# Attention, mixture of experts and SwiGLU: the low parts of the expert weights from the tenth tile on, on VectorE instead of GpSimd

## The chip, the cores and the metric

The kernel runs on one core of a Trainium2 chip. The metric is the device time of one execution in microseconds (us); the number for a version is the median of its runs. TensorE multiplies matrices, VectorE, ScalarE and GpSimd work on tiles element by element; GpSimd also issues the indirect transfers (gather and scatter), SyncE most of the plain ones. Each engine takes its instructions strictly in the order of its own queue, and waits for others by semaphores.

## The reference

Three stages in float32, the last with float64 weights:

```python
def reference(q, k, v, moe, moe2):          # q, k, v: 4 x 8 heads x 576 x 64
    scores = q @ k.T / 8                    # only the 64 latest positions of each row
    attn = softmax(where(mask, scores, -1e9)) @ v
    x = attn.reshape(2304, 512)
    noisy = x @ w_gate + log1p(exp(x @ w_noise)) * noise      # 8 experts
    top2 = two largest of noisy, w = softmax(top2)
    for e in range(8):                      # w1[e]: 512 x 1024, w2[e]: 1024 x 512
        for each token with e among its two:
            out[token] += w * (maximum(x[token] @ w1[e], 0) @ w2[e])
    g = out @ moe2_w_gate                   # 512 x 1536, float64 weights
    return (silu(g) * (out @ moe2_w_val)) @ moe2_w_out
```

## The kernel before

**Products in two parts.** Every large product is made of three faster ones. A number is split into a high part, rounded to the matrix format, and a low part, the remainder: high times high, high times low, low times high. So every weight tile of 128x1024 is loaded (tile `raw`, three buffers, L101), its high part copied (L116 on ScalarE, or L114 on GpSimd for the first nine), and its low part subtracted (L117). Both parts lie in a tile `wp` of nine buffers. There are 82 weight tiles: eight for each expert (four of w1, four of w2, tiles 0 to 63) and 18 of the last layer (tiles 64 to 81).

**The parts of the program.** Attention and routing come first; the first tiles are split in it. Then the expert layers (L849 to L904): the experts in turn, 0 to 7, the fullest first after expert 0, each with at most 640 to 576 token slots (`CAPS`). Then the last layer, SwiGLU, over 18 tiles of 128 tokens (L920 to L998).

**One expert.** `mm1` (L236) makes the hidden layer: for each f of 0 to 7, and for each of the two halves of the slots (256, then the remaining 320 to 384), twelve products (L248) into one of four PSUM banks, taken in turn. ScalarE writes the high part of the result (`ht`, L250) and VectorE the low part (L253); the bank is free for the fourth product group after it when both are done. `mm2` (L259) follows, five tiles t of 128 slots, 24 products each (L270). Between the tiles the gathered tokens of the next expert are turned, and their two parts written (L230 ScalarE, L233 VectorE).

**What is woven in.** The loop at L859 calls, after every `mm1` of one half, `decode_some(DEC1)`: one step of the decoding of the float64 weights of the last layer, of which there are seven for each half tile, all on VectorE (L143 to L157). After each f it calls `pump` (L169), which splits one more weight tile if a buffer has come free: in an expert's `mm1` this is so at f = 0 to 5 and 7, and once at the end of `mm2`, after t = 4. After each tile of `mm2`, `decode_some(DEC2)` gives six steps of decoding. In expert 0 steps of the routing (`finish_some`) stand where the decoding stands in the others; decoding runs in experts 1 to 6. At the start of an expert GpSimd gathers the next one's tokens (five transfers, L213), and in experts 1 to 3 it scatters 18 routing records, one after each f (L842, L843).

**What ties the splitting to the loads.** `split_pair` first asks for loads up to two tiles ahead, and a load waits in SyncE's queue until its `raw` buffer is free, that is until the low part of the tile three earlier has been subtracted.

The lines that the prediction speaks of are those of `split_pair` and these, from `mm1`'s caller:

```python
                    mm1(e, f, hf)()
                    if e:
                        decode_some(DEC1)
...
                pump()
```

Of the kernel before, what the change touches and what calls it, by code (L numbers as in the profile page):

```python
# [7 lines left out]
F32 = mybir.dt.float32  # L8
# [6 lines left out]
ALU = mybir.AluOpType  # L15
# [6 lines left out]
E = 8  # L22
# [4 lines left out]
KT = CT + 1  # L27
NW = 9
APAIRS = 8
# The slots of the first expert and of the others, the fullest first.  # L30
CAPS = (CAP, 640, 624, 608, 600, 592, 584, 576)
OFFS = tuple(sum(CAPS[:r]) for r in range(E + 1))
EARLY = 2
# [3 lines left out]
RNS, RNS2, RNS3, RT = 1300, 500, 1500, 13  # L37
NWARM, PSPL = 7, 9
EVP = {16: "da", 17: "da"}
# The steps after the last scores, in order: L logits, Q their turn, P turn of the weights, V weighted sum, X turn  # L40
# of x (each with its tile); G turn of gathered tokens, M first product, Y part of the second; W low parts; E, R
# routing on TensorE and VectorE.
TAIL = ("P16", "L14", "Q14", "R302", "X15", "R1500", "G0", "P17", "V16", "L15", "G1", "W", "V17", "Q15", "R9000", "X16",
        "M0", "L16", "X17", "R9000", "R500", "Q16", "R1", "R2500", "L17", "M2", "W", "R500", "M1", "Q17", "W", "M3",
        "R1500", "E", "R700", "M5", "M6", "M4", "R9000", "E", "W", "R9000", "Y0", "Y1", "M7")
# [8 lines left out]
def tile_attention_moe_swiglu(ctx: ExitStack, tc: tile.TileContext, qh, kh, vh, wgn, noise, w1h, w2h,  # L54
                              wg2, wv2, wo2, out):
    nc = tc.nc
# [12 lines left out]
    def bank(i, name, shape=None):  # L69
        return ps.tile(shape or [128, 512], F32, name=name, tag=f"b{i}")  # L70

# [1 line left out]
    srcs = []  # L73
    for r in range(E):
        srcs += [(r, w, j) for w in (w1h, w2h) for j in range(4)]
# [8 lines left out]
    NPAIR, WLIM = len(srcs), 8 * E + 6  # L84
# [3 lines left out]
    def load_pair():  # L88
        j = st["load"]
        if j >= NPAIR:  # L90
            return
        st["load"] += 1
        raws[j] = rp.tile([128, 1024], F32, name=f"raw{j}", tag="raw")
        src = srcs[j]
        if j < 8 * E:
            r, w, i = src
            if r and r not in rank_e:
                rank_e[r] = nc.values_load(rank_i[0:1, r:r + 1], engines=(mybir.EngineType.SP,), min_val=0,
                                           max_val=E - 1)
            src = w[bass.ds(rank_e[r], 1), i].rearrange("o p c -> p (o c)") if r else w[0, i]  # L100
        nc.sync.dma_start(raws[j], src)  # L101

    def split_pair(pool):
        j = st["split"]
        if j >= NPAIR:
            return
        while st["load"] < min(j + 3, st["lim"]):
            load_pair()
        st["split"] += 1
        w = pool.tile([128, 2, 1024], F32R, name=f"wp{j}", tag="w")  # L110
        pairs[j] = w
        r = raws.pop(j)
        if st["split"] <= PSPL:
            nc.gpsimd.tensor_scalar(w[:, 0, :], r, 1.0, 0.0, op0=ALU.mult, op1=ALU.add)  # L114
        else:
            nc.scalar.activation(w[:, 0, :], r, AF.Copy)  # L116
        (nc.gpsimd if j < WLIM or j % 2 else nc.vector).tensor_tensor(w[:, 1, :], r, w[:, 0, :].bitcast(F32), op=ALU.subtract)  # L117

    # The float64 weights of the last layer, rounded to float32 from their bits.
    TINY = 1.125 * 2.0 ** -15  # L120

    def decode_steps(pool):
# [46 lines left out]
    def pump():  # L169
        if st["split"] < min(st["used"] + NW - 1, st["lim"], WLIM):  # L170
            split_pair(wp)

# [1 line left out]
    nc.scalar.preload_act_table_set("natural_log_exp_and_others")  # L174
    init = rp.tile([128, 1024], I32, name="init", tag="raw")
    warm = nc.const_aps.tensor(1.0, (128, 1), BF)
# [80 lines left out]
    Y = {}  # L257
# [19 lines left out]
    def idx_x(e):  # L277
        return lambda t: idx_i[:, e * KT + t:e * KT + t + 1]

    # =============== attention and routing ===============  # L280
    with ExitStack() as ac:
        ap = ac.enter_context(tc.tile_pool(name="ap", bufs=1))

# [21 lines left out]
        Q, K, V, VW = {}, {}, {}, {}  # L305
# [291 lines left out]
        routing, at = [], {}  # L597

        def step():
            g = routing[0]  # L600
            at[g] = next(g, "end")
            if at[g] == "end":
                routing.pop(0)
            return at[g]

        def route_some(ns):
            """Emits routing steps of about ns on VectorE, and none that another engine has yet to answer."""
            while routing and ns > 0:
                r = step()
                if r in ("act", "pe", "dve"):  # L610
                    return
                if r != "end":
                    ns -= r if isinstance(r, int) else 220
# [29 lines left out]
        for T in range(NT - 2):  # L643
            trans_p(T)
            qk(T + 2, (0, 1))
            if T % 2 == 0 and T // 2 + 2 < NT // 2:
                load_super(T // 2 + 2)
            route_some(RNS if T < RT else RNS3)
            if T >= 2:
                logits(T - 2)  # L650
            if T >= 1:
                trans_x(T - 1)
            if T % 2 == 1 and T // 2 + 2 < NT // 2:
                link_k(T // 2 + 2)
            route_pe()
            route_some(RNS2 if T < RT else RNS3)
            qk(T + 2, (2,))
            if T >= 2:
                gates(T - 2)
            qk(T + 2, (3,))  # L660
            softmax(T + 2)
            pv(T)
            win_v(T + 2)
            route_pe()
            if T >= 3 and st["split"] < APAIRS:
                split_pair(wp)
        while routing:
            route_until("end")
        ops = {"L": logits, "P": trans_p, "Q": gates, "X": trans_x, "V": pv, "G": filler, "M": lambda f: filler(f + EARLY),
               "W": lambda _: lows(), "R": route_some, "E": lambda _: route_pe(),  # L670
               "Y": lambda k: mm2(0, k // 4, hp_, "xg", range(2 * (k % 4), 2 * (k % 4) + 2))}
        for op in TAIL:
# [12 lines left out]
        nc.vector.tensor_copy(pos_c, pos_ps)  # L685
        nc.scalar.preload_act_table_set("sigmoid_and_others")

    # =============== expert layers ===============
    GY, XC, X2 = {}, {}, {}

    def gather(T, g0, g1, slots, rows):
# [26 lines left out]
    def finish(pool):  # L718
        V = nc.vector

        def ft(name, shape, dt=F32):
            return pool.tile(shape, dt, name=name)

        def wide(a, shape):
            return a.to_broadcast(shape)

        # The experts but the first in the order of their tokens, the fullest first: isr[r, e].
        key = ft("key8", [128, E])
        V.scalar_tensor_tensor(key, cnt, float(E), kb, op0=ALU.mult, op1=ALU.add)
        yield  # L730
        isr = ft("isr", [128, E, E])
# [7 lines left out]
                        op=ALU.is_equal)  # L739
# [15 lines left out]
        yield  # L755
        V.tensor_copy(idx_i.rearrange("p (e t) -> p e t", t=KT)[:, 1:, 0:CT], idm[:, 1:])
        yield "idx"
        # Too many tokens for an expert's slots?
        V.tensor_tensor(tmp, isr, wide(cnt[:, None, :], [128, E, E]), op=ALU.mult)
        yield  # L760
        ovr = ft("ovr", [128, E])
# [6 lines left out]
        yield  # L768
        V.tensor_tensor(cnt_i, cm[0:1, :], few[0:1, :], op=ALU.max)
        yield  # L770
        # The tokens in the order of the last layer: those of the last expert come after the others, the last tile
        # stays in its place.
        big = ft("big", [128, NT, E])
        lastp, lasto = ft("lastp", [128, NT]), ft("lasto", [128, NT])
        for src, dst in ((pos_c, lastp), (ohs, lasto)):
# [13 lines left out]
        yield  # L789
        V.tensor_copy(ord_i[:, NT - 1:NT], rec[:, NT - 1:NT, 4])  # L790
        yield
        # Slots.
        off = ft("off", [128, E])
        V.tensor_tensor(tmp, isr.rearrange("p r e -> p e r"), wide(offs[:, None, :], [128, E, E]), op=ALU.mult)
        yield
# [3 lines left out]
        for c in range(2):  # L799
            V.tensor_tensor(big, wide(io8[:, None, :], [128, NT, E]), wide(mf_all[:, :, c:c + 1], [128, NT, E]),  # L800
                            op=ALU.is_equal)
# [25 lines left out]
    with ExitStack() as mc:  # L827
# [3 lines left out]
        dec.append(decode_steps(mp))  # L831

        st_, fin = [], finish(mp)

        def finish_some(n):
# [69 lines left out]

    outer.close()

    # =============== SwiGLU ===============
    with ExitStack() as sc:
        sp = sc.enter_context(tc.tile_pool(name="sp", bufs=1))  # L910
        ep = sc.enter_context(tc.tile_pool(name="ep", bufs=len(m2) - NW))
# [8 lines left out]
        while st["split"] < WLIM:  # L920
            split_pair(wp)
# [4 lines left out]
        for bk in range(NBK):  # L926
# [18 lines left out]
            for h in range(2):  # L945
                ut = sp.tile([128, 2, 6, NB2], F32R, name=f"ut{bk}_{h}", tag="ut")
                for fi in range(6):
                    f = 6 * h + fi
                    gb = []
                    for kind in ("g", "v"):  # L950
                        w = pairs[mi[kind, f // 2]].rearrange("p s (k f) -> p s k f", k=NK)
# [26 lines left out]
                order = [(fi, i) for i in range(3) for fi in range(6)] if end else \  # L978
                    [(fi, i) for fi in range(6) for i in range(3)]
                for fi, i in order:  # L980
                    f = 6 * h + fi
                    w = pairs[mi["o", f // 2]].rearrange("p s (c d) -> p s c d", c=2)
# [14 lines left out]
                for i in range(3):  # L997
                    put_out(i)  # L998

    # =============== an expert with more tokens than its slots: every token through every expert ===============  # L1000
    fp = ctx.enter_context(tc.tile_pool(name="fp", bufs=1))
    rv = nc.values_load(cnt_i[0:1, 0:1], min_val=0, max_val=8 * N)
    with tc.If(rv > 0):
# [105 lines left out]
```

## Time and profile before

| what | us |
|---|---|
| median of three runs | 1088.21 |
| the three runs | 1087.7, 1088.21, 1090.81 |
| profiled execution: span, first to last instruction | 1084.2 |
| TensorE busy (matmul) | 1027.2 (95%) |
| VectorE busy | 609.1 (56%) |
| ScalarE busy | 340.2 (31%) |
| GpSimd busy | 334.5 (31%) |
| L117, low parts, on GpSimd | 185.2 in 76 instructions |
| L117, low parts, on VectorE | 7.4 in 6 instructions |

Of the profiled execution the profile gives the span only; the median of the runs is 4.0 us above it. The profile's views give, for a stretch or an instruction, the start in us from the span's beginning, the duration, the engine (PE is TensorE, DVE VectorE, ACT ScalarE, POOL GpSimd, SPq SyncE's queue), the line, and the tile written and read. Idle time before an instruction is put down to what ended it. A duration includes whatever the instruction stood still for after it had started.

### The profile page before, as it was taken

To read this page: it belongs to the slowest core of one execution; us is meant where nothing else is said; L and a number is where in the kernel's file an instruction comes from. 1 tells how busy PE (TensorE), PEld (TensorE's weight loads), DVE (VectorE), ACT (ScalarE), POOL (GpSimd) and SP (SyncE) were. 2 spreads that over 40 slices of the span, in tenths; PEclk is the share of its full clock that TensorE was granted. 3 is DMA by queue.
4 is the path that set the end of the run, shared out by engine and by line. 5 is a ranking of instruction groups with operands and counts; after the bars stand their busy time and mean duration, and the time that the engine had idled before them with its cause. 6 is when DMAs were issued, how large, how long until landed. Compare 5 with 4: busy or idle time off the path is not lost.

```text
span 1084.2 us, 16995 instructions
## 1 busy us (share of the span) xinstructions
PE 1027.2 (95%) x6754; PEld 917.8 (85%) x6754; DVE 609.1 (56%) x1094; ACT 340.2 (31%) x808; POOL 334.5 (31%) x293
## 2 busy tenths in 40 slices
PE   8978999799797999989899999999999999999997
PEld 5656788789687888888879799999999999999996
DVE  4688846878889697888924253433424324324321
ACT  6856524423323242333324162212212212212211
POOL 2653115935717063452708153300300201100000
PEclk9989999999998999999999999999999999999999
DMA  7853115747566375655616162200200201100000
GB/s 240 299 187 99 60 53 191 232 123 244 137 197 198 135 247 167 209 175 188 218 59 191 68 217 79 88 1 1 88 1 1 88 1 34 56 1 2 29 1 32
DMA packets 55774, 125.63 MB, mean 116 GB/s; under 512 B 9144, under 2 KB 19512, under 8 KB 55688
## 3 DMA queue, kind: packets, MB, share of 16 engines
q1 hardware_dynamic: 40695, 87.72, 25.5%
q0 software_dynamic: 7936, 23.91, 6.9%
q10 hardware_dynamic: 7056, 12.85, 3.2%
q8 instruction: 55, 0.90, 0.3%
q14 instruction: 32, 0.25, 0.1%
HBM read 95.57 MB, written 28.88 MB: 115 GB/s over the span
## 4 chain that ended last, share of the span: by engine, by line
PE 80%; DVE 14%; ACT 2%; DMA 1%; issue 1%; SPq 1%; POOL 0%; ACTq 0%; DVEq 0%
PE y L270 20%; PE g L958 14%; PE v L958 14%; PE o L986 14%; PE h L248 12%; DVE da L143 2%; PE gt L228 2%; PE xp L445 1%; DVE da L153 1%; DVE db L151 1%; DVE db L155 1%; DVE ht L253 1%; DVE da L157 1%; DVE da L145 1%; PE sc L404 1%
## 5 line engine op out<-in xcount | busy, mean ns | idle before, releaser
L117 POOL TENSOR_TENSOR wp<-raw,wp 128x1024 fp32r<-128x1024 f32 x76 | 185.2, 2447 | 249.0 <-ACT wp L116 241.9
L248 PE MATMUL h<-xh,wp 128*128 128x256 f32 (+6 forms) x1536 | 229.8, 310 | 29.0 <-DVE ht L253 28.8
L248 PEld LDWEIGHTS h<-xh,wp 128*128 128x128 f32 x1536 | 222.5, 195 | 35.7 <-DVE ht L253 34.1
L270 PE MATMUL y<-wp,ht 128*128 128x512 f32 (+6 forms) x960 | 228.9, 394 | 0.0
L270 PEld LDWEIGHTS y<-wp,ht 128*128 128x128 f32 (+6 forms) x960 | 172.4, 183 | 40.5
L958 PE MATMUL g<-x,wp 128*128 128x384 f32 x864 | 161.6, 334 | 0.0
L958 PE MATMUL v<-x,wp 128*128 128x384 f32 x864 | 161.3, 334 | 0.0
L986 PE MATMUL o<-wp,ut 128*128 128x512 f32 x648 | 153.6, 392 | 0.0
L958 PEld LDWEIGHTS g<-x,wp 128*128 128x128 f32 x864 | 151.3, 188 | 1.0
L958 PEld LDWEIGHTS v<-x,wp 128*128 128x128 f32 x864 | 150.8, 188 | 0.0
L986 PEld LDWEIGHTS o<-wp,ut 128*128 128x128 f32 x648 | 120.4, 188 | 24.1
L963 DVE TENSOR_TENSOR eg<-g,eg 128x384 f32<-128x384 f32 x72 | 40.2, 558 | 151.8 <-ACT eg L962 151.7
L693 POOL DMA_INDIRECT gy<-y_d,recp x30 | 28.7, 955 | 214.3 <-DVE xc L700 206.5
L116 ACT ACTIVATE wp<-raw 128x1024 fp32r<-128x1024 f32 x73 | 76.7, 1055 | 54.8 <-DMA raw<-in_w_dram 37.7
L250 ACT ACTIVATE ht<-h 128x256 fp32r<-128x256 f32 (+7 forms) x128 | 52.7, 421 | 113.3 <-PE h L248 107.1
L966 ACT ACTIVATE ut<-u 128x384 fp32r<-128x384 f32 x72 | 37.9, 526 | 148.2 <-DVE u L965 148.2
L253 DVE SCALAR_TENSOR_TENSOR ht<-h,ht 128x256 fp32r<-128x256 f32 (+7 forms) x128 | 59.1, 465 | 35.6 <-ACT ht L250 35.5
L274 ACT ACTIVATE ys<-y 128x512 f32<-128x512 f32 (+6 forms) x40 | 23.9, 597 | 171.2 <-PE y L270 129.9
L965 DVE TENSOR_TENSOR u<-v,eg 128x384 f32<-128x384 f32 x72 | 40.2, 558 | 62.8 <-PE v L958 62.1
L962 ACT ACTIVATE eg<-g 128x384 f32<-128x384 f32 x72 | 35.3, 490 | 125.7 <-PE g L958 125.7
L233 DVE TENSOR_TENSOR xh<-gt,xh 128x512 fp32r<-128x512 f32 (+6 forms) x40 | 25.7, 662 | 70.5 <-ACT xh L230 70.5
L967 DVE TENSOR_TENSOR ut<-u,ut 128x384 fp32r<-128x384 f32 x72 | 40.9, 568 | 43.0 <-ACT ut L966 43.0
(184 smaller groups left out, 1023.0 us busy)
## 6 DMA issues: line engine op xcount, KB each, us to landing
raw<-in_w_dram SPq DMA_DIRECT2D x64, 512.0 KB, 4.2
w_d<-da ACTq DMA_DIRECT2D x36, 256.0 KB, 3.5
raw<-w_d SPq DMA_DIRECT2D x18, 512.0 KB, 3.4
y_d<-ys SPq DMA_DIRECT2D x34, 256.0 KB, 2.2
rd<-in_wg_dram SPq DMA_DIRECT2D x12, 512.0 KB, 4.7
rd<-in_wv_dram SPq DMA_DIRECT2D x12, 512.0 KB, 4.4
rd<-in_wo_dram SPq DMA_DIRECT2D x12, 512.0 KB, 4.0
v<-in_v_dram SPq DMA_DIRECT2D x18, 256.0 KB, 6.2
```

What stands on the lines that cost most here:

```text
L116: nc.scalar.activation(w[:, 0, :], r, AF.Copy)
L117: (nc.gpsimd if j < WLIM or j % 2 else nc.vector).tensor_tensor(w[:, 1, :], r, w[:, 0, :].bitcast(F32), op=ALU.subtract)
L248: nc.tensor.matmul(b_, w[:, a, k, fc], xh[:, c, k, 0:m], start=(n == 0), stop=(n == 11))
L250: nc.scalar.activation(ht[:, 0, f, 0:m], b_, AF.Relu)
L253: nc.vector.scalar_tensor_tensor(ht[:, 1, f, 0:m], b_, 0.0, ht[:, 0, f, 0:m].bitcast(F32), op0=ALU.max, op1=ALU.subtract)
L270: nc.tensor.matmul(b_, ht[:, a, f, sl], w[:, c, f % 2, :], start=(f == 0 and n == 0), stop=(f == 7 and n == 2))
L958: nc.tensor.matmul(b_, w[:, a, k, fc], x2[:, c, k, :], start=(n == 0), stop=(n == 11))
L963: nc.vector.tensor_tensor(eg, gb[0], eg, op=ALU.mult)
L965: nc.vector.tensor_tensor(u, gb[1], eg, op=ALU.mult)
L966: nc.scalar.activation(ut[:, 0, fi, :], u, AF.Copy)
L967: nc.vector.tensor_tensor(ut[:, 1, fi, :], u, ut[:, 0, fi, :].bitcast(F32), op=ALU.subtract)
L986: nc.tensor.matmul(ob[i], ut[:, a, fi, sl], w[:, c, f % 2, :], start=(f == 0 and n == 0), stop=(f == 11 and n == 2))
```

## The change

One expression decides the engine of the low part of weight tile j. `WLIM` is 70 and `PSPL` is 9. Before, GpSimd took all tiles below 70 and the odd ones of the last twelve. Now GpSimd takes tiles 0 to 8 and the odd ones of the last twelve; tiles 9 to 69, 61 in all, go to VectorE.

```diff
@@ -114,9 +114,9 @@
             nc.gpsimd.tensor_scalar(w[:, 0, :], r, 1.0, 0.0, op0=ALU.mult, op1=ALU.add)
         else:
             nc.scalar.activation(w[:, 0, :], r, AF.Copy)
-        (nc.gpsimd if j < WLIM or j % 2 else nc.vector).tensor_tensor(w[:, 1, :], r, w[:, 0, :].bitcast(F32), op=ALU.subtract)
+        (nc.gpsimd if j < PSPL or (j >= WLIM and j % 2) else nc.vector).tensor_tensor(w[:, 1, :], r, w[:, 0, :].bitcast(F32), op=ALU.subtract)
```

The rest of the diff takes out comments. The queues of TensorE, ScalarE and SyncE keep their instructions and their order. Three places in the queues of the other two engines follow.

VectorE at the end of expert 2 and the start of expert 3. `wp` is the weight tile that is split, `da` and `db` are the decoding's tiles, `ht_0` and `ht_1` the hidden layer's two halves; the row of `wp_3937` is the split after t = 4 of `mm2`.

```order
 L143 TENSOR_SCALAR da_0_3903<-rd_0_3854 128x512
 L145 SCALAR_TENSOR_TENSOR da_0_3903<-rd_0_3854,da_0_3903 128x512
+L117 TENSOR_TENSOR wp_3937<-raw_3634,wp_3937 128x1024
 L149 TENSOR_SCALAR db_0_3904<-da_0_3903 128x512
 L151 SCALAR_TENSOR_TENSOR db_0_3904<-rd_0_3854,db_0_3904 128x512
@@ -501,24 +521,30 @@
 L253 SCALAR_TENSOR_TENSOR ht_1_3978<-h_0_1_3979,ht_1_3978 128x352
 L149 TENSOR_SCALAR db_1_3949<-da_1_3948 128x512
+L117 TENSOR_TENSOR wp_3998<-raw_3708,wp_3998 128x1024
 L253 SCALAR_TENSOR_TENSOR ht_0_3961<-h_1_0_4003,ht_0_3961 128x256
 L151 SCALAR_TENSOR_TENSOR db_1_3949<-rd_1_3901,db_1_3949 128x512
 L253 SCALAR_TENSOR_TENSOR ht_1_3978<-h_1_1_4019,ht_1_3978 128x352
```

A subtraction now stands ahead of the last six decoding steps of an expert, and one behind the second half of each f but f = 6, ahead of the next f's `ht`.

VectorE in expert 0, f = 4 to 7 of `mm1`. The rows of L764 to L786 are steps of the routing.

```order
 L767 TENSOR_REDUCE cm<-ovr 128x1
 L769 TENSOR_TENSOR cnt_i<-cm,few 1x1
+L117 TENSOR_TENSOR wp_2580<-raw_2552,wp_2580 128x1024
 L253 SCALAR_TENSOR_TENSOR ht_1_2449<-h_5_1_2583,ht_1_2449 128x384
 L776 TENSOR_TENSOR big<-pos_c,isr 128x144
 L778 TENSOR_REDUCE lastp<-big 128x18
 L776 TENSOR_TENSOR big<-ohs,isr 128x144
+L117 TENSOR_TENSOR wp_2606<-raw_2554,wp_2606 128x1024
 L253 SCALAR_TENSOR_TENSOR ht_1_2449<-h_6_1_2609,ht_1_2449 128x384
 L778 TENSOR_REDUCE lasto<-big 128x18
```

Tiles 9 and 10 are now subtracted ahead of `ht` of f = 5 and f = 6.

GpSimd in expert 0 and at the start of expert 1; `xg` are the gathered tokens, `rec_d` the routing records.

```order
 L114 TENSOR_SCALAR wp_2556<-raw_2540 128x1024
 L117 TENSOR_TENSOR wp_2556<-raw_2540,wp_2556 128x1024
-L117 TENSOR_TENSOR wp_2580<-raw_2552,wp_2580 128x1024
-L117 TENSOR_TENSOR wp_2606<-raw_2554,wp_2606 128x1024
-L117 TENSOR_TENSOR wp_2649<-raw_2578,wp_2649 128x1024
-L117 TENSOR_TENSOR wp_2796<-raw_2604,wp_2796 128x1024
 L213 DMA xg_0_2799<-x_d,idx_i 128x512
 L213 DMA xg_1_2801<-x_d,idx_i 128x512
```

From tile 8 on GpSimd's queue in the expert layers holds only gathers, scatters and the one-element memsets between them.

## Rows read from the trace of the kernel before

**Rows 1.** The page's part 1: busy us (share of the span) xinstructions, TensorE.

```profile
PE 1027.2 (95%) x6754; PEld 917.8 (85%) x6754; DVE 609.1 (56%) x1094; ACT 340.2 (31%) x808; POOL 334.5 (31%) x293
```

**Rows 2.** The waits: engine, line <- releaser: total us, times, longest us.

```profile
ACT wp L116 <- DMA raw<-in_w_dram: 37.7, 16, 6.0
...
PE h L248 <- DVE ht L253: 28.8, 17, 6.2
```

**Rows 3.** Windows, `mm1` of experts 1 to 7: stretch, its length, each engine's busy us.

```profile
187.66:224.23 36.57, 29.69 (x195) 28.20 (x194) 30.92 (x30) 13.94 (x24) 29.97 (x26) 1.00 0.66 194
...
253.79:289.33 35.54, 29.99 (x193) 28.80 (x192) 34.44 (x34) 13.32 (x23) 30.41 (x26) 0.95 0.73 221
...
318.88:355.50 36.62, 30.11 (x194) 29.61 (x193) 34.56 (x36) 13.26 (x23) 24.84 (x16) 0.86 0.72 224
...
384.99:416.22 31.23, 27.38 (x193) 26.61 (x192) 30.30 (x34) 13.28 (x23) 22.85 (x12) 1.00 0.78 245
...
445.71:476.91 31.20, 28.41 (x194) 27.79 (x192) 31.01 (x34) 13.12 (x23) 23.14 (x12) 0.95 0.72 238
...
506.42:537.83 31.41, 28.03 (x194) 27.19 (x192) 30.98 (x34) 13.20 (x23) 23.03 (x12) 0.95 0.75 251
...
567.55:593.15 25.60, 25.60 (x193) 25.59 (x192) 8.29 (x14) 13.25 (x23) 19.72 (x11) 1.00 0.56 175
```

**Rows 4.** Timeline of TensorE: start us, us, x products; first unbroken run of each `mm1`.

```profile
187.66 19.80 PE L248 MATMUL h<-xh,wp 128*128 128x256 f32 x132
...
253.79 20.77 PE L248 MATMUL h<-xh,wp 128*128 128x256 f32 x144
...
318.88 18.39 PE L248 MATMUL h<-xh,wp 128*128 128x256 f32 x132
...
384.99 16.79 PE L248 MATMUL h<-xh,wp 128*128 128x256 f32 x120
...
445.71 16.56 PE L248 MATMUL h<-xh,wp 128*128 128x256 f32 x120
...
506.42 16.35 PE L248 MATMUL h<-xh,wp 128*128 128x256 f32 x120
```

**Rows 5.** Timeline of VectorE in `mm1` of experts 1 and 3.

```profile
222.14 0.41 DVE L253 SCALAR_TENSOR_TENSOR ht<-h,ht 128x256 fp32r<-128x256 f32 x1
...
224.14 0.41 DVE L253 SCALAR_TENSOR_TENSOR ht<-h,ht 128x256 fp32r<-128x256 f32 x1
...
324.73 0.68 DVE L145 SCALAR_TENSOR_TENSOR da<-rd,da 128x512 int32<-128x512 int32 x1
...
337.47 8.12 DVE L145 SCALAR_TENSOR_TENSOR da<-rd,da 128x512 int32<-128x512 int32 x1
345.51 0.41 DVE L253 SCALAR_TENSOR_TENSOR ht<-h,ht 128x256 fp32r<-128x256 f32 x1
```

**Rows 6.** Timeline of GpSimd in `mm1` of expert 3.

```profile
323.74 1.25 POOL L213 DMA_INDIRECT xg<-x_d,idx_i  x1
...
338.05 6.98 POOL L117 TENSOR_TENSOR wp<-raw,wp 128x1024 fp32r<-128x1024 f32 x3
```

**Rows 7.** One line, L117: xcount: duration ns min/median/max, first and last start us.

```profile
L117 POOL TENSOR_TENSOR wp<-raw,wp x76: 2336/2406/2954, 36.0 to 654.7; 128x1024 fp32r<-128x1024 f32 x76
...
L117 DVE TENSOR_TENSOR wp<-raw,wp x6: 1225/1226/1227, 629.7 to 653.7; 128x1024 fp32r<-128x1024 f32 x6
```

**Rows 8.** Timelines in expert 3 (ScalarE) and expert 0 (ScalarE, GpSimd, TensorE).

```profile
319.62 1.05 ACT L116 ACTIVATE wp<-raw 128x1024 fp32r<-128x1024 f32 x1
...
168.22 1.06 ACT L116 ACTIVATE wp<-raw 128x1024 fp32r<-128x1024 f32 x1 [0.70 <-DMA raw<-in_w_dram]
...
170.14 9.50 POOL L117 TENSOR_TENSOR wp<-raw,wp 128x1024 fp32r<-128x1024 f32 x4
...
169.15 5.65 PE L270 MATMUL y<-wp,ht 128*128 128x512 f32 x24
```

**Rows 9.** DMA issues: queue, xcount, KB each, median us from issue to landing.

```profile
raw<-in_w_dram SPq DMA_DIRECT2D x64, 512.0 KB, 4.2
```

## The prediction

> **What bounds the kernel now.** First the busy shares: TensorE works 95% of the span [rows 1], so only the stretches where it stands still can be won. Next the waits: the only large wait of TensorE is that of the hidden layer's products (L248) for VectorE's low part of an earlier result (L253), 28.8 us in 17 times [rows 2]; the product needs one of four PSUM banks, and VectorE has not emptied it. Next the windows: `mm1` takes 36.57, 35.54, 36.62, 31.23, 31.20 and 31.41 us in experts 1 to 6, and 25.60 in expert 7, which does the same number of products on slightly fewer columns [rows 3]. Expert 7 has no decoding; VectorE is busy 8.29 us there, against 30.30 to 34.56 in the others, where it fills the stretch nearly whole [rows 3]. So in `mm1` of experts 1 to 6 VectorE is the bound. `mm2` and the last layer show no such waits.
>
> How much TensorE loses there I take from its unbroken run at the start of each `mm1`, before the banks run out, scaled to the 192 products of the stage [rows 4]: 19.80 x 192/132 = 28.80, 20.77 x 192/144 = 27.69, 18.39 x 192/132 = 26.75, 16.79 x 1.6 = 26.86, 16.56 x 1.6 = 26.50, 16.35 x 1.6 = 26.16; together 162.76. The six windows sum to 202.57. **The loss is 39.8 us.** (Scaled by columns from expert 7's 25.60, the clean sum is 162.1 and the loss 40.5.) It is above the 28.8 of the wait view, since products after a standstill also run slower: in expert 3, with the longest one, the granted clock is 0.86 of full in the mean, a share of its time at the lower of the two levels [rows 3].
>
> Is VectorE's busy time work? The same decoding instruction (L145, 128x512) takes 0.68 us at 324.73 and 8.12 us at 337.47 [rows 5]. Beside the second GpSimd runs three low-part subtractions from 338.05 to 345.03 [rows 6], and the instruction ends half a microsecond after them. Behind it in VectorE's queue stands the `ht` of L253, which then takes its plain 0.41 us [rows 5]. Beside the first there is a gather's issue on GpSimd (323.74 to 324.99) [rows 6], and it does no harm. So the decoding steps stand still while GpSimd subtracts; VectorE's long hours are mostly that.
>
> **The change, part by part.** *Removed from GpSimd:* 61 subtractions of 2.41 us [rows 7], 147 us of GpSimd time that nothing waits for directly. What goes with them is the standstill of VectorE. What remains on GpSimd in experts 1 to 6 are gathers and scatters.
>
> *Added to VectorE:* 61 subtractions of 1.23 us, as the six in the last layer [rows 7]; about 75 us of work, of which 7 in each `mm1`. Does it fit? One f without a subtraction and without standstill takes VectorE 2.00 us (222.14 to 224.14: two `ht`, two decoding steps) [rows 5]. With one it is 3.23, and TensorE's f takes 28.80/8 = 3.60 in expert 1 down to 26.16/8 = 3.27 in expert 6, where the `ht` are narrower too. So VectorE fits with little to spare, and the products hide it. A subtraction among the expert layers on VectorE is not in this trace. From below 1.23 bounds it. From above I take GpSimd's 2.41: then an f needs 4.41, a stage 8 x 4.41 - 2.41 = 32.9 us (one f has none), and experts 1 to 3 win 9.9 while 4 to 6 lose 4.9: 5 us faster. I take 1.23: same engine, shapes and types.
>
> *The wait added at each stage's start.* The subtraction after t = 4 stands ahead of six decoding steps, and waits for ScalarE's high part, which comes after the last result of `mm2`. In expert 3 that high part ends at 319.62 + 1.05 = 320.67 [rows 8], 1.8 us after `mm1` began. Then 1.23 for the subtraction, six steps of at most 0.68 (4.1, the short ones among them make it about 3.6), and the first `ht`, 0.41 [rows 5]: done at 325.9. TensorE wants that bank again after four product groups, 318.88 + 26.75/4 = 325.57. It waits about 0.35 us, similarly in experts 2 and 4 to 6 (0.1 to 0.5). **Cost: 2.0 us.** Afterwards VectorE keeps pace as above. In expert 1 routing stands in place of the decoding, and no such wait arises.
>
> *Expert 0.* Tile 10's high part is done at 168.22 + 1.06 = 169.28, but GpSimd still subtracts tile 8 from 170.14 on (first of the four in 9.50 us) [rows 8], and I let VectorE stand behind it until 172.5. Then subtraction to 173.7, `ht` of f = 6 to 174.2, f = 7 a good microsecond later. TensorE's `mm2` tile from 169.15 (24 products, 5.65 us) [rows 8] wants f = 6 at its 20th product, 173.6, and f = 7 at the 23rd. **Cost: 1.2 us**, between 0 and 2.
>
> *Edits that cost nothing.* Loads: a `raw` buffer is now freed after 1.23 us on VectorE instead of after GpSimd's pile of three; a load lands 4.2 us after issue [rows 9], and is asked for three f, some 10 us, ahead. GpSimd's gathers no longer stand behind subtractions and start earlier. Tiles 60 to 69 fall where VectorE is nearly idle (8.29 of 25.60) [rows 3].
>
> A rule against the change, weighed by itself: the rows say that most of VectorE's busy time in `mm1` is standstill. The Trainium skill, "Perfetto Trace Analysis", section "Optimizing Scalar/DVE Operations", says that from a saturated VectorE work may be moved to ScalarE or even GpSimd, the reverse of this edit; it adds that the two share an SBUF read port, so that moving work between them may not help. By the first half the sum would be a loss (the second rival below), by the second about nothing; by the rows it is a gain of 36.6. The trace speaks against the first half, with 0.68 against 8.12 us for one instruction.
>
> **Sum.** -39.8 + 2.0 + 1.2 = -36.6 us against the profiled span of 1084.2: 1047.6. The median lies 4.0 above that span, and the work outside the span is not touched: 1088.2 - 36.6 = **1051.6**, rounded 1052.
>
> **Rivals.**
> *Loads set the pace.* VectorE's subtraction now waits, with all behind it, for a weight tile's load; ScalarE waited 37.7 us in 16 times for these loads, up to 6.0 [rows 2]. For it: the same bytes in shorter stages, and the DMA engines are already busy 0.66 to 0.78 of them [rows 3]. Against: those loads were late because GpSimd freed the buffers late. The loop is subtraction, load, high part, three tiles apart: 1.23 + 4.2 + 1.05 = 6.5 us, against three f of 9.8 to 10.8. It bites once a landing takes over 7.5 us. At 9 us, three tiles take 11.3, eight 30.1: against 27.1 clean in the mean, 3.0 lost in each of six stages, 18 us of the gain: about 1070. Above roughly 10.4 us (8/3 x 12.7 = 33.8, the present mean) the kernel gets slower.
> *VectorE's busy time is work.* Then `mm1` of experts 1 to 6 is what VectorE shows now, 192.2 us [rows 3], plus 6 x 7 x 1.23 = 51.7: 243.9 against 202.6, 41 us slower: 1129. It decides where an f on VectorE exceeds TensorE's present 31.41/8 = 3.93 us, that is where the rest beside the subtraction takes over 2.7 us instead of 2.00. Against it stand the paired durations [rows 5]. (This is the case that the first half of the rule of the Trainium skill, "Perfetto Trace Analysis", has in view.)
> *The standstill only changes place,* behind gathers and scatters or the subtraction at the stage's start: that would need some 6 us in each of six stages where I find 0.35: about 1088. The 0.68 us beside a gather speaks against it.
> That the change does not do what it says is excluded by the queues: 61 rows leave GpSimd, 61 come to VectorE.
>
> **How the numbers follow.** Forecast (1046 to 1060) 0.75; loads set the pace, faster still (1060 to 1080) 0.13; standstill moved, within 0.3% (3.3 us, about what a measurement here can tell from no change) 0.04; VectorE's time is work, or loads above 10.4 us, slower, 0.08. Faster 0.88, same 0.04, slower 0.08. The range for 8 in 10: below, 1046, all of 40.5 won and a little of the spread of runs (1.5); above, 1072, a good half of the gain lost to loads.
>
> **What would show it.** Right: `mm1` of experts 1 to 6 at 26 to 29.5 us each; VectorE's decoding steps all near 0.7 us, none of several us; L117 on VectorE near 1.23; TensorE's wait for L253 down from 28.8 to a few us; stages of `mm2` and the last layer as before. Wrong: L253 waiting behind an L117 that waits for ScalarE and a load (loads set the pace), stretched L117 or decoding beside gathers (standstill moved), or an f on VectorE above 3.6 us with unstretched instructions (it is work).

## The result, and the profile after

The changed kernel takes 1049.58 us (median of four runs, 1047.69 to 1052.27), the kernel before 1087.95 beside it (1083.37 to 1090.81). The ratio is 0.9665, with a 95% interval of 0.9633 to 0.9697: 38 us or 3.4% faster. The profiled execution took 1050.45 us with a span of 1048.7, so 35.5 us less span than before; the prediction's sum was made on spans, and said 36.6.

The first part of the page after, the line that answers to [rows 1]:

```profile
PE 1019.6 (97%) x6754; PEld 912.6 (87%) x6754; DVE 570.3 (54%) x1155; ACT 340.0 (32%) x808; POOL 185.0 (18%) x232
```

VectorE was given 61 subtractions, 74.6 us more of L117 than before (82.0 against 7.4), and is busy 38.8 us less. So, if the rest of its work is the same, some 113 us of what looked like VectorE's work before was standstill.

The waits after, in the columns of [rows 2]:

```profile
DVE wp L117 <- ACT wp L116: 33.9, 21, 6.3
...
ACT wp L116 <- DMA raw<-in_w_dram: 18.1, 9, 7.7
...
PE h L248 <- DVE ht L253: 2.3, 5, 0.6
```

TensorE's wait for L253 fell from 28.8 to 2.3 us. VectorE does wait for ScalarE's high part now (first line); most of that costs TensorE nothing, and what it costs at the stages' starts is taken up below.

The windows of `mm1` in experts 1 to 7 after, in the columns of [rows 3]:

```profile
189.03:218.21 29.18, 28.60 (x196) 28.24 (x194) 22.43 (x38) 13.88 (x24) 9.78 (x17) 1.00 0.70 216
...
247.76:276.13 28.37, 28.00 (x194) 27.40 (x192) 24.96 (x43) 13.43 (x23) 7.31 (x11) 1.00 0.79 227
...
305.67:332.95 27.28, 27.14 (x193) 26.84 (x192) 25.11 (x43) 13.25 (x23) 0.00 (x0) 1.00 0.77 248
...
362.44:389.53 27.09, 26.88 (x194) 26.59 (x192) 25.06 (x43) 13.31 (x23) 0.00 (x0) 1.00 0.82 252
...
419.02:446.10 27.08, 26.50 (x194) 26.22 (x192) 25.00 (x43) 13.04 (x23) 0.00 (x0) 1.00 0.73 241
...
475.61:502.28 26.67, 26.16 (x194) 25.89 (x192) 23.79 (x41) 13.07 (x23) 0.00 (x0) 1.00 0.71 236
...
532.00:557.60 25.60, 25.60 (x193) 25.59 (x192) 15.85 (x24) 13.23 (x23) 7.27 (x6) 1.00 0.67 225
```

Experts 1 to 6 sum to 165.67 us against 202.57: 36.9 us won, all of it here. The granted clock is 1.00 in each of them; before it was 0.86 to 0.95 in experts 2, 3, 5 and 6, and 1.00 in experts 1 and 4, though TensorE stood still there too [rows 3]. Expert 7 takes 25.60 as before, though VectorE does twice its work there. The books close: `mm1` -36.90, expert 0 +0.72 (from the start of its `mm1` to that of expert 1: 35.98 against 35.26), attention +0.65 (its `mm1` began at 153.05 against 152.40); together -35.53, and the last layer begins 35.55 us earlier.

The decoding step of [rows 5] and the subtraction of [rows 7] after, all instructions of a line: xcount, duration in ns min/median/max:

```profile
L145 DVE SCALAR_TENSOR_TENSOR da<-rd,da x36: 681/692/699, 198.3 to 510.3; 128x512 int32<-128x512 int32 x36
```

```profile
L117 DVE TENSOR_TENSOR wp<-raw,wp x67: 1212/1226/1237, 168.1 to 617.6; 128x1024 fp32r<-128x1024 f32 x67
```

No step of L145 takes more than 0.70 us now, where the longest took 8.12, and each subtraction takes the 1.23 that was put in the sum.

### The profile page after: what moved, and what is told of

Its sections match the earlier page's. It is cut to its first block, busy times and chain, and to the rows that moved or that the text cites. A ratio compares the mean times of both kernels' runs of the same rounds, so it can differ in the third digit from the quotient of the medians.

```text
span 1048.7 us, 16938 instructions
## 1 busy us (share of the span) xinstructions
PE 1019.6 (97%) x6754; PEld 912.6 (87%) x6754; DVE 570.3 (54%) x1155; ACT 340.0 (32%) x808; POOL 185.0 (18%) x232
## 4 chain that ended last, share of the span: by engine, by line
PE 85%; DVE 7%; DMA 3%; issue 2%; ACT 2%; SPq 1%; ACTq 0%; POOL 0%; DVEq 0%
PE y L270 20%; PE h L248 15%; PE g L958 14%; PE v L958 14%; PE o L986 14%; PE xp L445 2%; PE gt L228 2%; PE ptp L185 1%; PE sc L404 1%; DMA w_d<-da 1%; PE ct L185 1%; DVE wp L117 1%; DMA rd<-in_wg_dram 1%; DVE nm L414 1%; ACT wp L116 1%
## 5 line engine op out<-in xcount | busy, mean ns | idle before, releaser
L248 PE MATMUL h<-xh,wp 128*128 128x256 f32 (+6 forms) x1536 | 219.5, 303 | 2.4 <-DVE ht L253 2.3
L248 PEld LDWEIGHTS h<-xh,wp 128*128 128x128 f32 x1536 | 215.5, 190 | 5.9 <-DVE ht L253 4.3
L117 DVE TENSOR_TENSOR wp<-raw,wp 128x1024 fp32r<-128x1024 f32 x67 | 82.0, 1225 | 35.4 <-ACT wp L116 33.9
L213 POOL DMA_INDIRECT xg<-x_d,idx_i x38 | 36.7, 967 | 283.0 <-PE gt L228 239.7
L116 ACT ACTIVATE wp<-raw 128x1024 fp32r<-128x1024 f32 x73 | 76.6, 1054 | 24.5 <-DMA raw<-in_w_dram 18.1
L962 ACT ACTIVATE eg<-g 128x384 f32<-128x384 f32 x72 | 35.3, 490 | 126.3 <-PE g L958 126.3
L253 DVE SCALAR_TENSOR_TENSOR ht<-h,ht 128x256 fp32r<-128x256 f32 (+7 forms) x128 | 60.3, 474 | 17.3 <-ACT ht L250 17.3
```

The lines of the kernel that those rows point to most:

```text
L117: (nc.gpsimd if j < PSPL or (j >= WLIM and j % 2) else nc.vector).tensor_tensor(w[:, 1, :], r, w[:, 0, :].bitcast(F32), op=ALU.subtract)
L248: nc.tensor.matmul(b_, w[:, a, k, fc], xh[:, c, k, 0:m], start=(n == 0), stop=(n == 11))
L253: nc.vector.scalar_tensor_tensor(ht[:, 1, f, 0:m], b_, 0.0, ht[:, 0, f, 0:m].bitcast(F32), op0=ALU.max, op1=ALU.subtract)
```

## The experiments

The question was what the 37 us were. **Standstill:** VectorE's decoding steps stand still while GpSimd subtracts. **Late loads,** the rival that the change cannot tell apart by itself: GpSimd, with its subtractions behind gathers and scatters, frees the `raw` buffers late, so weight tiles come late and ScalarE, VectorE and TensorE after them. Four kernels on one chip, where the kernel before took 1085.78 us (seven runs).

### More buffers for the loads, subtractions on GpSimd

```diff
-    rp = ctx.enter_context(tc.tile_pool(name="rp", bufs=3))
+    rp = ctx.enter_context(tc.tile_pool(name="rp", bufs=4))
...
-        while st["load"] < min(j + 3, st["lim"]):
+        while st["load"] < min(j + 4, st["lim"]):
```

> The kernel before (all tiles below 70 on GpSimd) with four raw buffers instead of three, and loads asked for three tiles ahead instead of two. Theory (standstill: a VectorE decoding step stands still while GpSimd subtracts): the subtractions stay on GpSimd, so the decoding steps of several us stay and the time is that of before, 1083 to 1091 us; ScalarE's waits for the loads (37.7 us) fall, but that is not the bound. Rival (late loads: what the change won is that raw buffers come free sooner): most of the gain is had here too, 1050 to 1065 us, and TensorE's wait for L253 (28.8 us) falls to under 10.

Measured: 1100.29 us (1097.11 to 1101.47), ratio 1.0129 (1.0107 to 1.0151): 1.3% slower, and above the 1083 to 1091 that the standstill had expected. Its waits:

```profile
PE h L248 <- DVE ht L253: 42.0, 13, 8.5
...
ACT wp L116 <- DMA raw<-in_w_dram: 6.9, 6, 2.5
```

The waits for loads fell from 37.7 to 6.9 us, so the remedy for late loads worked, and TensorE waits longer for VectorE than before. Late loads fall as a theory. That it would be slower neither theory had said. The timelines of GpSimd and VectorE in expert 3, and all steps of one decoding line, show where it comes from:

```profile
336.16 9.28 POOL L117 TENSOR_TENSOR wp<-raw,wp 128x1024 fp32r<-128x1024 f32 x4
```

```profile
335.59 10.40 DVE L145 SCALAR_TENSOR_TENSOR da<-rd,da 128x512 int32<-128x512 int32 x1
```

```profile
L153 DVE TENSOR_TENSOR da<-da,db x36: 673/692/12665, 195.7 to 561.0; 128x512 f32<-128x512 f32 x36
```

With tiles ready sooner, four subtractions stand in a row on GpSimd instead of three, and one decoding step stands through all four: 10.40 us in place of 8.12. In experts 4 to 6 five stand in a row, a step stands 12.3 to 12.7 us, and `mm1` takes 35.3 to 35.9 us instead of 31.2 to 31.4 [rows 3]. The four PSUM banks cover four product groups, 26.75/4 = 6.7 us in expert 3; what a standstill has beyond that reaches TensorE. That a row is worse than the same number apart is not shown. Against the version without waits (below), a stage with its seven subtractions loses 8.6 and 8.1 us in experts 1 and 2 of this run, where they come one by one; experts 4 to 6 lose 4.6 to 5.5 us in the kernel before, with rows of three and two, and 9.2 to 9.4 us here, with rows of five.

### Every second tile back on GpSimd

```diff
-        (nc.gpsimd if j < PSPL or (j >= WLIM and j % 2) else nc.vector).tensor_tensor(w[:, 1, :], r, w[:, 0, :].bitcast(F32), op=ALU.subtract)
+        (nc.gpsimd if j < PSPL or j % 2 else nc.vector).tensor_tensor(w[:, 1, :], r, w[:, 0, :].bitcast(F32), op=ALU.subtract)
```

> The kernel after with the odd ones of tiles 9 to 69 back on GpSimd (31 of 61). Theory (standstill): every second tile brings a standstill of about 2.4 us again; the four PSUM banks cover part of it, so between a quarter and two thirds of the 36.9 us that mm1 won is lost: 1058 to 1075 us. VectorE's decoding steps show a second length of 2 to 3.5 us, hardly any of 8, since three subtractions no longer stand in a row. Rival (late loads): with every second subtraction on VectorE no pile forms on GpSimd, buffers are free in time, under 1055 us.

Measured: 1062.50 us (1057.73 to 1065.47), ratio 0.9793 (0.9777 to 0.9810). TensorE waits 10.6 us for L253, and `mm1` of experts 1 to 6 sums to 175.3 us by the starts of the stages in TensorE's timeline: 9.6 of the 36.9 us are lost again, at half the number of subtractions. The decoding's longest step:

```profile
L153 DVE TENSOR_TENSOR da<-da,db x36: 672/691/2796, 199.9 to 519.5; 128x512 f32<-128x512 f32 x36
```

2.8 us, one subtraction long, and none of 8, as the standstill has it.

### GpSimd busy with reading, and freeing nothing

```diff
+    dummy = cp.tile([128, 1024], F32, name="dummy")
+    nc.gpsimd.memset(dummy, 0.0)
...
+        if PSPL <= j < WLIM:
+            nc.gpsimd.tensor_tensor(dummy, dummy, w[:, 0, :].bitcast(F32), op=ALU.subtract)
```

> The kernel after with one more GpSimd instruction for each of tiles 9 to 69: a subtraction of 128x1024 between the tile's high part and a scratch tile of its own, whose result nothing uses. It frees no raw buffer and no load waits for it. Theory (standstill): decoding steps and also the low parts on VectorE stand still beside it, VectorE's hours grow by some 61 x 2.4 us less what misses them, and the time is back at 1075 us or more, possibly above the kernel before. Rival (late loads): the loads are as in the kernel after, 1047 to 1055 us.

Measured: 1124.90 us (1124.22 to 1127.61), ratio 1.0357 (1.0339 to 1.0374): 39 us slower than the kernel before, and about 75 slower than the changed one, for instructions that nothing waits for. In expert 3, GpSimd and VectorE (the lines of this kernel are two to four further down; L155 is a decoding step):

```profile
342.29 2.39 POOL L121 TENSOR_TENSOR dummy<-dummy,wp 128x1024 f32<-128x1024 f32 x1
```

```profile
341.64 3.59 DVE L155 SCALAR_TENSOR_TENSOR db<-rd,db 128x512 f32<-128x512 uint32 x1
345.16 0.51 DVE L257 SCALAR_TENSOR_TENSOR ht<-h,ht 128x352 fp32r<-128x352 f32 x1
```

The decoding step begins before GpSimd's instruction and ends half a microsecond after it. TensorE waits 56.1 us for the `ht` behind such steps, more than the 28.8 of before; VectorE now has the low parts besides. The loads land in 4.4 us in the median, no later than in the changed kernel (4.7). The standstill is shown, by itself.

### GpSimd busy with writing

```diff
+        if PSPL <= j < WLIM:
+            nc.gpsimd.tensor_tensor(dummy[0:1, 0:1], dummy[0:1, 0:1], w[0:1, 0, 0:1].bitcast(F32), op=ALU.subtract)
+            for _ in range(2):
+                nc.gpsimd.memset(dummy, 0.0)
```

> As the run with the reading GpSimd instruction, but for each tile GpSimd reads one element of the high part (so that it starts at the same time) and then twice sets the scratch tile of 128x1024 to zero, about 2 us in which it only writes. Theory in its plain form (any busy GpSimd holds VectorE): as with the reading instruction, 1075 us or more. Theory in its narrow form (what GpSimd reads is what holds VectorE's steps with two operands in SBUF): those keep 0.69 us and L117 1.23, only the single-operand steps L143 and L149 may be held; 1047 to 1060 us. The Trainium skill, SBUF — State Buffer, section Who interferes with whom, states the narrow form.

Measured: 1048.23 us (1046.38 to 1052.22), ratio 0.9663 (0.9638 to 0.9688), as the changed kernel. GpSimd's memsets, and a decoding step with two operands and one with a single one:

```profile
L123 POOL MEMSET dummy<- x122: 951/956/1133, 171.1 to 589.1; 128x1024 f32 x122
```

```profile
L149 DVE TENSOR_SCALAR da<-rd x36: 407/420/1215, 191.9 to 500.6; 128x512 int32<-128x512 int32 x36
L151 DVE SCALAR_TENSOR_TENSOR da<-rd,da x36: 673/687/693, 192.7 to 506.7; 128x512 int32<-128x512 int32 x36
```

119 us of memsets (the reading instructions took 167) leave L151 (two operands in SBUF) at its 0.69; only the single-operand steps are held, up to 1.3 us, about one memset long. So what holds a step with two operands in SBUF is not a busy GpSimd, but what GpSimd reads. The Trainium skill, "SBUF — State Buffer", section "Who interferes with whom", says so: a VectorE instruction with two SBUF inputs contends with a GpSimd instruction that reads SBUF, not with one that only writes. These two runs agree.

Steps with a single operand stand beside GpSimd's subtractions as well. In the kernel before:

```profile
L143 DVE TENSOR_SCALAR da<-rd x36: 408/419/7743, 194.4 to 539.6; 128x512 int32<-128x512 int32 x36
```

The Trainium skill, "SBUF — State Buffer", section "Summary: rules for kernel authors", also says that the second to issue stands until the first is through. The trace does not settle that. In the run with the reading instruction GpSimd's, begun 0.12 us after a subtraction on VectorE, took 3.36 us, as if it stood for it:

```profile
331.55 1.22 DVE L119 TENSOR_TENSOR wp<-raw,wp 128x1024 fp32r<-128x1024 f32 x1 [2.02 <-ACT wp L118]
```

```profile
331.67 3.36 POOL L121 TENSOR_TENSOR dummy<-dummy,wp 128x1024 f32<-128x1024 f32 x1 [25.18 <-ACT wp L118]
```

But where a decoding step stood, it too had begun first, some 0.6 us ahead of GpSimd (341.64 against 342.29). And it stood through three, four and five GpSimd instructions in a row (8.12, 10.40 and 12.66 us), so the end of one is too short a wait to reckon with.

### What is left, and a faster version

In the changed kernel TensorE still waits five times in experts 1, 2, 4, 5 and 6, 0.2 to 0.6 us each. Four kernels on another chip (before: 1087.01 us, eleven runs), the changed kernel among them.

> The changed kernel itself once more, beside the three that follow, so that they are compared on one chip: 1047 to 1053 us.

Measured: 1048.28 us, ratio 0.9646 (0.9619 to 0.9672); `mm1` of experts 1 to 6 sums to 166.1 us.

The subtraction after t = 4 behind the decoding steps:

```diff
-                pump()
                 if e:
                     decode_some(DEC2)
                 else:
                     finish_some(FIN2)
+                pump()
```

> The kernel after with pump() moved behind the decoding steps of an mm2 tile, so that the subtraction after t = 4 no longer stands ahead of six decoding steps. Theory (the wait at the start of each stage is this subtraction's place): the waits of 0.2 to 0.6 us in experts 2 to 6 go, 1 to 2 us are won: ratio to before 0.001 to 0.002 lower than that of the kernel after. Rival (these waits are late loads or stores): nothing changes.

Measured: 1045.90 us, ratio 0.9629 (0.9604 to 0.9654). The totals' intervals overlap; the stages decide. Experts 4 to 6 take 26.60, 26.24 and 25.91 us, against 27.08, 27.07 and 26.68: the wait at their start is gone, 0.5 to 0.8 us each. Expert 3 got slower, 27.72 against 27.28. Its timeline on VectorE:

```profile
308.29 0.43 DVE L143 TENSOR_SCALAR da<-rd 128x512 int32<-128x512 int32 x1 [2.31 <-DMA w_d<-da]
308.63 1.22 DVE L117 TENSOR_TENSOR wp<-raw,wp 128x1024 fp32r<-128x1024 f32 x1
```

Decoding, now earlier, runs into the store of its own result, of which there are two buffers.

The store three steps later, and a third buffer:

```diff
-            a = pool.tile([128, 512], I32, name=f"da{j}_{hf}", tag="da", bufs=2)
+            a = pool.tile([128, 512], I32, name=f"da{j}_{hf}", tag="da", bufs=3)
...
-            if done is not None:
-                nc.scalar.dma_start(*done)
             V.tensor_scalar(b, a, -0x00800000, None, op0=ALU.bitwise_and)
...
             V.tensor_tensor(af, af, bf, op=ALU.add)
             yield
+            if done is not None:
+                nc.scalar.dma_start(*done)
```

> As the run with the decoding first, and the store of a decoded half is issued three decoding steps later on ScalarE's queue, with three buffers da instead of two. Theory: in the kernel after, ScalarE stands 2 to 3 us at a stage's start for VectorE's last decoding step of the half that it is to store, ahead of its ht; with VectorE less behind this wait falls under 1 us, and TensorE loses nothing any more: another 0 to 1 us won. Rival: the wait is covered by the four banks, no difference.

Measured: 1046.17 us, ratio 0.9625 (0.9600 to 0.9650); expert 3 takes 26.88 us, the six stages 162.1 instead of 163.4. ScalarE's waits for decoding steps ahead of its `ht` (9.4 us after, 2.9 with the decoding first) no longer appear among its longest.

All low parts below tile 70 on VectorE:

```diff
-        (nc.gpsimd if j < PSPL or (j >= WLIM and j % 2) else nc.vector).tensor_tensor(w[:, 1, :], r, w[:, 0, :].bitcast(F32), op=ALU.subtract)
+        (nc.gpsimd if (j >= WLIM and j % 2) else nc.vector).tensor_tensor(w[:, 1, :], r, w[:, 0, :].bitcast(F32), op=ALU.subtract)
```

> The kernel after with the low parts of tiles 0 to 8 on VectorE too; GpSimd keeps the high part of these tiles and the odd low parts of the last twelve. Theory (standstill): VectorE's routing steps in attention no longer stand still beside nine subtractions of 2.4 us, but VectorE gets nine of 1.23, and it is on TensorE's path there; expert 0 wins back its 0.7 us, since tile 8 no longer holds GpSimd at 170 to 172.5. In sum -4 to +3 us against the kernel after. Rival (VectorE is the bound in attention, whatever GpSimd does): 5 us or more slower than the kernel after.

Measured: 1050.76 us, ratio 0.9667 (0.9641 to 0.9692), no faster. Expert 0 takes 40.08 us instead of 35.71, since VectorE stands for tile 8's high part, which waits on GpSimd behind gathers:

```profile
167.58 1.22 DVE L117 TENSOR_TENSOR wp<-raw,wp 128x1024 fp32r<-128x1024 f32 x1 [7.47 <-POOL wp L114]
```

Expert 0's `mm1` began at 149.92, against 151.20 in the changed kernel's run beside it; so nothing shows that attention suffered, though this start varies by more than that (below). The part of the theory on expert 0 failed.

Three more on a third chip (before: 1087.29 us, nine runs). First the decoding ahead of the subtraction once more:

> The kernel with the decoding ahead of the subtraction once more, beside the two that follow: 1045 to 1048 us.

Measured: 1051.60 us, ratio 0.9666 (0.9645 to 0.9686), outside what was expected, on the same kernel. In its profiled execution expert 0's `mm1` began at 155.56 instead of 150.94; from there to the last layer it is 431.8 us, against 430.8. Of the 5.6 us between the two spans, 4.6 lie in attention, whose code is the same.

The first load of the decoding asked for in advance:

```diff
         nxt = fetch(0)
+        yield
         done = None
...
         dec.append(decode_steps(mp))
+        decode_some(1)
```

> As the run with the late store, and the first load of the decoding is asked for before expert 0's last products instead of in expert 1. Theory: in all kernels so far VectorE stands 4 to 5 us in expert 1 for this load, with ht behind it; in the kernel after that costs TensorE 0.6 us, which go: mm1 of expert 1 at 28.4 to 28.7 instead of 29.2 us, the whole at 1045 to 1046 us. Rival: the load is then late for something else in expert 0 (the weight tiles' loads behind it on SyncE's queue), no gain.

Measured: 1047.67 us (1045.23 to 1050.29), ratio 0.9638 (0.9615 to 0.9661), above the 1045 to 1046 that was expected; expert 1 came out as the theory had it. The windows of `mm1` in experts 1, 2 and 6:

```profile
190.63:218.95 28.32, 28.32 (x195) 28.19 (x194) 23.24 (x38) 13.93 (x24) 12.34 (x17) 1.00 0.71 209
248.52:275.99 27.47, 27.47 (x193) 27.47 (x192) 25.23 (x43) 13.42 (x23) 7.34 (x11) 1.00 0.81 251
...
473.85:499.75 25.90, 25.90 (x193) 25.89 (x192) 24.52 (x43) 13.31 (x23) 0.00 (x0) 1.00 0.75 253
```

Length and TensorE's busy time are equal in each: the six stages take 161.42 us, and TensorE stands for nothing. VectorE is busy 24.5 of 25.90 us in expert 6, so it only just keeps up.

On top of that all low parts below tile 70 on VectorE, tile 8's high part on ScalarE:

```diff
-        if st["split"] <= PSPL:
+        if st["split"] <= APAIRS:
```

> As the run with the early first load, with all low parts of tiles 0 to 69 on VectorE, and tile 8's high part on ScalarE instead of GpSimd, where it stands behind five gathers. Theory: in the run with all low parts on VectorE the attention was faster by about 1 us, and expert 0 slower by 4.3, since VectorE stood 7.5 us for that high part; without this, 1 to 3 us faster than the kernel without the two moves: 1042 to 1045 us. Rival: VectorE is the bound in attention, no gain or a loss of 1 to 3 us.

Measured: 1045.94 us (1044.48 to 1048.44), ratio 0.9628 (0.9606 to 0.9650), 1.7 us below the run beside it, though not under the 1045 that was expected. Expert 0 takes 35.29 us instead of 36.16 in the run beside it, `mm1` is the same, and attention ended 1.1 us sooner, which is within its spread (below). In its stages this is the fastest version; beside the changed kernel (0.9646 and 0.9665 in two measurements) the totals show 2 to 4 us with overlapping intervals. The kernel with the decoding first came out at 0.9629 and at 0.9666, so as a total the gain is not settled.

## Why the prediction was right

**The loss and its place.** 39.8 us were read out of [rows 4] and [rows 3] as lost in six stages, with clean stages of 162.76 us. Measured by the version without any wait, 161.42, the loss was 41.1; scaling the first unbroken runs came out 1.3 high, and scaling by columns from expert 7 (162.1) was nearer.

**VectorE's time is standstill, not work.** Right, shown by the reading and the writing GpSimd. The rival that it is work would have given 1129 us. A busy share of 30.98 in 31.41 us [rows 3] said saturated, and the durations of one instruction said otherwise. (The advice of the Trainium skill, "Perfetto Trace Analysis", section "Optimizing Scalar/DVE Operations", to move some work from a saturated VectorE to ScalarE or even GpSimd would have been the wrong one here: VectorE was not saturated, and the opposite move made the kernel 3.4% faster. The page's own caution, that the two share an SBUF read port and that moving work between them might not help, is in line with that.)

**The added subtractions fit.** 1.23 us each, as put (by the upper bound of 2.41 us, experts 1 to 3 would have won 10.0 us and not 9.9, a slip that changes nothing); VectorE fills 23.79 of 26.67 us in expert 6. Loads land in 4.7 us in the median instead of 4.2, under the 7.5 at which they would bite; ScalarE's waits for them halved.

**The wait at a stage's start.** Put at 0.1 to 0.5 us in each of experts 2 to 6, 2.0 in all. In expert 3 the timelines give, ScalarE first:

```profile
306.41 1.05 ACT L116 ACTIVATE wp<-raw 128x1024 fp32r<-128x1024 f32 x1
```

```profile
307.50 1.23 DVE L117 TENSOR_TENSOR wp<-raw,wp 128x1024 fp32r<-128x1024 f32 x1 [2.00 <-ACT wp L116]
...
312.22 0.42 DVE L253 SCALAR_TENSOR_TENSOR ht<-h,ht 128x256 fp32r<-128x256 f32 x1
```

The first `ht` ends 6.97 us after `mm1` began at 305.67; 7.0 was put. TensorE's products show no gap here, but a weight load stood for it:

```profile
312.69 1.49 PEld L248 LDWEIGHTS h<-xh,wp 128*128 128x128 f32 x12 [0.43 <-DVE ht L253]
```

In experts 4, 5 and 6 TensorE stood 0.21, 0.58 and 0.52 us at its 49th product, the place that was named. Moving the subtraction took these waits away. In expert 2 its 0.37 us came at the 97th product, behind 1.45 us in which VectorE waited for the store of a decoded half, which was not put. Against the version without waits, `mm1` of experts 2 to 6 takes 0.90, 0.39, 0.48, 0.85 and 0.77 us more: 3.4 in all, where 2.0 was put. What else the prediction left out: ScalarE stood at the same place for the decoding's last step, which it was to store.

**Expert 0.** Put at 1.2 us, measured 0.72. VectorE and TensorE:

```profile
171.31 1.21 DVE L117 TENSOR_TENSOR wp<-raw,wp 128x1024 fp32r<-128x1024 f32 x1
172.45 0.55 DVE L253 SCALAR_TENSOR_TENSOR ht<-h,ht 128x384 fp32r<-128x384 f32 x1
...
174.82 0.55 DVE L253 SCALAR_TENSOR_TENSOR ht<-h,ht 128x384 fp32r<-128x384 f32 x1
```

```profile
175.43 0.73 PE L270 MATMUL y<-wp,ht 128*128 128x512 f32 x2 [0.41 <-DVE ht L253]
```

Tile 10's subtraction began at 171.31, not 172.5. TensorE stood for the `ht` of f = 7 alone, ahead of its 23rd product, 0.41 us, as placed. Another execution of the changed kernel has expert 0 at 35.71 us, 0.45 above the kernel before.

**Expert 1,** where no wait was put, lost 0.58 us: VectorE stood 4.99 us for the decoding's first load (4.16 before the change), and with the subtraction besides the banks no longer covered it. The load asked for in advance took it away (28.32 us against 29.05 in the version that lacks only this).

**The step from span to time** was weak: 4.0 us were put between a span of 1084.2 and a median of 1088.2. The changed kernel's own span lies 1.75 us below its own time, so most of those 4 us were the difference of one execution from the median. The sum held within 1.1 us on spans, in part because its errors have opposite signs: the loss was 1.3 us larger than put, but so was the cost in the six stages, by 2.2 (4.2 us in place of 2.0); expert 0 cost 0.5 less, and attention came out 0.65 later, which lies within its spread. That the terms are right is shown by the stages, not by so close a total.

## What to carry to other kernels

A busy engine may be standing still inside its instructions: before an engine is called saturated, compare the durations of one instruction, of one shape, at times when the others differ. An instruction on GpSimd that reads SBUF can stop VectorE's steps that read SBUF alone, although no semaphore joins them, and the price shows where VectorE's queue is awaited next; moving that work to VectorE was cheaper for VectorE itself (1.23 us of work for up to 2.9 of standstill beside one subtraction, 3.59 us in place of 0.69). And another buffer, which let such instructions gather in longer rows, made it worse.

## What the runs showed of the hardware that was not expected

One VectorE step stood through a whole row of GpSimd subtractions, 8.12 us through three, 10.40 through four and 12.66 through five. The `ht` steps, which read one operand from PSUM, kept their time amid such rows; in the kernel before, GpSimd first:

```profile
464.73 5.38 POOL L117 TENSOR_TENSOR wp<-raw,wp 128x1024 fp32r<-128x1024 f32 x2 [0.63 <-ACT wp L116]
```

```profile
467.77 0.41 DVE L253 SCALAR_TENSOR_TENSOR ht<-h,ht 128x256 fp32r<-128x256 f32 x1
```

Two memsets of 128x1024 per tile on GpSimd, 119 us in all, cost nothing measurable (1048.23 us). The same attention code ended at 150.9 us in one profiled execution and at 155.6 in another (the start of expert 0's `mm1`), with a granted clock of 0.90 and 0.83 between 50 and 100 us; this spread is as large as all that the later versions won in the expert layers, and it limits what a total can resolve here.
